# Probabilities transposed by the DMA crossbar instead of by TensorE, in a windowed-attention plus rational-MLP kernel

## The chip, the cores and the metric

The kernel runs on one core of a Trainium2 chip. The metric is the device time of one execution in microseconds (us). The core has TensorE (PE, with its weight loads as PEld), VectorE (DVE), ScalarE (ACT), GpSimd (POOL), SyncE (SP, which here only issues transfers) and 16 DMA engines.

## The reference

Eight sequences of 576 positions, eight heads of width 64, a causal window of 128 keys with a linear bias; then a two-layer network whose activation is a ratio of polynomials.

```python
scores = scale * np.matmul(q, k.transpose(0, 1, 3, 2))
rel = pos[:, None] - pos[None, :]
mask = (rel >= 0) & (rel < 128)
scores = np.where(mask, scores + bias[None], -1000000000.0)
attn = np.exp(scores - np.max(scores, axis=-1, keepdims=True))
attn = attn / (np.sum(attn, axis=-1, keepdims=True) + 1e-09)
x = np.matmul(attn, v)                  # to (4608 tokens, 512)
h = x @ w_in                            # 512 x 2048
P = a[0] + a[1] * h + a[2] * h**2 + a[3] * h**3
Q = 1.0 + np.abs(b[0]) * np.abs(h) + np.abs(b[1]) * h**2
out = (P / (Q + 1e-6)) @ w_out          # 2048 x 512
```

## The kernel before

The 4608 tokens are cut into 18 tiles of 256. Each tile has two attention jobs (function `attention`, j = 0 to 35), one for each half of the heads; a job has two units (function `unit`, i = 0, 1), each with two heads and two blocks of 128 tokens. The MLP (function `mlp`) then takes the tile in 8 pairs of 128-wide slices of the hidden layer. Attention of the next tile stands between the matmuls of the MLP of this tile, so one tile holds two jobs. The stretch from one job to the next is called a half of a tile below.

A job begins on PE with one block of small matmuls: the value products of the job before (`side<-p_all` and `side<-p_far`, L397), then its own scores (`sc<-kq` and `side<-kq`, L444). DVE merges the scores (L468) and takes their maximum with the bias (L507), eight instructions in a job; ACT takes the exponentials (L512), eight in a job; DVE makes the reciprocal of the sum (L519, L520); POOL multiplies (`pr<-pr,st`, L521). PE then transposes the probabilities `pr` of a unit by four matmuls against an identity (L536) into PSUM, ACT copies them out (`p_all`, L539), and POOL splits them by two instructions into `p_far` (L543) and the rest (L544).

A pair of the MLP: PE makes `h` (L621); ACT makes `g_u` (L635) and `g_p` (L649); POOL makes `g_q` (L636, L650); ACT takes a logarithm (L653) and an exponential (L654); DVE makes `g_h` (L656) and `g_l` (L659), which PE multiplies with the second weights (`acc`, L676). Matmuls in three parts of fp32r keep the precision. In the first tile the weights still arrive as 64-bit floats, and ACT and DVE turn them into fp32 (L582 to L584).

No order is written by hand: every operation is handed to a list scheduler (`Plan`) with a due time from a table of numbers and a cost, and each engine's program is emitted in the order that it finds. Each engine then runs its list in that order, so an instruction that waits holds up those behind it. SP issues nearly all transfers, from one queue.

Of the kernel before, what the change touches and what calls it, by code (L numbers as in the profile page):

```python
# [15 lines left out]
U32 = mybir.dt.uint32  # L16
AF = mybir.ActivationFunctionType
# [18 lines left out]
EARLY = 0  # L36

# [42 lines left out]
class Plan:  # L80
# [34 lines left out]
    def order(self):  # L115
# [76 lines left out]
        while n < total:  # L192
# [12 lines left out]
            for e in "pavgsq":  # L205
                while free_at[e] <= t:
# [7 lines left out]
                    if best is None:  # L214
                        break
# [54 lines left out]
def banded_attention_ratio_mlp(ctx: ExitStack, tc: tile.TileContext, kqv, w_in, w_out, ab, bias, ident, out):  # L270
# [14 lines left out]
    A0, DA, T0, L0, L1 = -4.313, 1.223, 17.768, 62.357, 26.153  # L285
    AOFF, D2, D3, JL, VL = -0.7979, 3.783, 6.667, 12.545, 6.301
    SP, SV, SA, SG, LL = 0, 0.3731, 0.1218, 0.3643, 2.215
    ML, ZA, ME, OE, C0 = 25.673, 0.5894, 1.484, 12.272, 0.9828
    DC, CO, DO, WL, S0 = 4.041, 22.113, 3.584, 5.75, 81.852
    DS, SL, AW, BL, VE = 1.47, 9.066, 23.44, 0.2145, 5.594  # L290
    DU, V0, DL = 0.8139, 7.94, 1.703
# [11 lines left out]
    def act(n, psum, ptr=0):  # L303
        return (67 if psum else 105) + 0.833 * n + 95 * ptr
# [7 lines left out]
    masks = slot(const, [P, 2, P], F32, "masks")  # L312
    masks16 = slot(sb3, [P, 2, P], BF16, "masks16", tag="p_far")
# [44 lines left out]
    def job(j, i):  # L358
# [24 lines left out]
    stage = {}  # L383

# [34 lines left out]
    def attention(j):  # L419
# [4 lines left out]
        side = [slot(ps4, [P, 2, 2, P], F32, f"side{h}", tag="h") for h in range(2)]  # L424
# [6 lines left out]
        extra = lambda h: ap(side[h])[:, 0].rearrange("q i (b c) -> q i b c", b=2)  # L431
# [14 lines left out]
        if t == 0:  # L446
            for i in range(2):
                plan.op(A + DU * i, {"p": 290 + 664}, lambda e, i=i: scores(i), reads=jobs[i][3], writes=mk + [(side[0], 0), (side[1], 0)], rows=0.9)
# [18 lines left out]
        for h in range(2):  # L467
# [4 lines left out]
                reads=[mk[h], (side[h], 0), (masks, 0)], writes=[mk[h]])  # L472
# [10 lines left out]
    def unit(j, i, A, main, mk, pt, v):  # L483
# [54 lines left out]
        plan.op(A + D2, {"p": 28 + 108 * 4}, transpose, reads=[(pr, y) for y in range(4)] + [(id_sb, 0)], writes=pk)  # L538
# [243 lines left out]
```

## Time and profile before

| | |
|---|---|
| time, median of 3 runs (lowest to highest) | 999.61 us (999.29 to 1000.06) |
| time of the profiled execution | 999.67 us |
| its span | 997.9 us |
| busy: PE, DVE, ACT, POOL | 98%, 79%, 61%, 53% |

The profiled execution lies 0.06 us above the median, and its span 1.8 us below its time. The engines work at the same time, so the shares don't add up; a busy PE can still have matmuls that overlap.

### The profile page before, as it was taken

The page shows a single profiled execution, that of the slowest core. Times are in us where ns is not written, and L with a number is a line of the kernel's source. Part 1 is how long each engine was busy: PE and PEld are TensorE (multiplying, and loading weights), DVE is VectorE, ACT ScalarE, POOL GpSimd, SP SyncE. Part 2 cuts the span into 40 slices and gives each one's busy share as a digit, 9 for nine tenths or more (in the row PEclk, how much of TensorE's full clock was granted, in tenths as well). Part 3 has the DMA queues.
Part 4 walks back from the last instruction along what each step waited for, and adds up shares of the span by engine and source line. Part 5 has one row for each costly group of instructions (what it writes and reads, how often), then busy time and mean ns, then how long its engine had stood idle before and what let it go on. Part 6 is the DMA issues. An engine that isn't in the chain of part 4 may idle for free.

```text
span 997.9 us, 25220 instructions
## 1 busy us (share of the span) xinstructions
PE 976.8 (98%) x9999; PEld 867.0 (87%) x9999; DVE 791.6 (79%) x1786; ACT 611.6 (61%) x1410; POOL 525.4 (53%) x529
## 2 busy tenths in 40 slices
PE   6899899999999999999999999999999999999998
PEld 4756698999999999999999999999999999999997
DVE  5799997887878787877787877878787878777775
ACT  5798865665656566655656565656566565656452
POOL 3448984555555554554545454555555545545332
PEclk7899999999999999999999999999999999999999
DMA  9991311121112112121212131203021221200000
GB/s 283 366 325 26 95 48 60 50 94 41 62 51 74 56 54 70 49 75 55 70 49 75 39 96 45 79 2 102 22 80 44 55 75 54 71 1 22 2 22 22
DMA packets 54502, 73.86 MB, mean 74 GB/s; under 512 B 5488, under 2 KB 38512, under 8 KB 54384
## 3 DMA queue, kind: packets, MB, share of 16 engines
q1 hardware_dynamic: 53664, 71.59, 22.9%
q8 instruction: 79, 1.29, 0.6%
q10 hardware_dynamic: 720, 0.66, 0.2%
q14 instruction: 39, 0.32, 0.1%
HBM read 62.79 MB, written 9.44 MB: 72 GB/s over the span
## 4 chain that ended last, share of the span: by engine, by line
PE 91%; DVE 3%; DMA 3%; ACT 1%; issue 1%; SPq 0%; ACTq 0%; DVEq 0%
PE h L621 40%; PE acc L676 39%; PE side L397 5%; PE sc L536 3%; PE sc L444 3%; PE side L444 1%; DMA v<-in_kqv 1%; DVE w L584 1%; DMA kq<-in_kqv 1%; DMA raw<-in_w_in 1%; DMA bias_std<-in_bias 1%; ACT pr L512 0%; DVE cv L583 0%; DVE g_q L644 0%; DVE g L647 0%
## 5 line engine op out<-in xcount | busy, mean ns | idle before, releaser
L621 PE MATMUL h<-x_hi,hi 128*128 128x256 f32 x1088 | 313.6, 288 | 0.0
L621 PE MATMUL h<-x_hi,lo 128*128 128x256 f32 x1088 | 306.2, 281 | 0.0
L621 PE MATMUL h<-x_lo,hi 128*128 128x256 f32 x1088 | 306.0, 281 | 0.0
L636 POOL TENSOR_SCALAR g_q<-g_u,babs 128x512 f32<-128x512 f32 x144 | 123.2, 855 | 252.8 <-ACT g_u L635 252.1
L621 PEld LDWEIGHTS h<-x_lo,hi 128*128 128x128 f32 x1088 | 204.7, 188 | 43.1 <-issue 1.0
L621 PEld LDWEIGHTS h<-x_hi,hi 128*128 128x128 f32 x1088 | 205.3, 189 | 25.4 <-issue 0.7
L676 PE MATMUL acc<-lo,g_h 128*128 128x512 f32 x544 | 214.7, 395 | 0.0
L676 PE MATMUL acc<-hi,g_h 128*128 128x512 f32 x544 | 214.5, 394 | 0.0
L676 PE MATMUL acc<-hi,g_l 128*128 128x512 f32 x544 | 207.7, 400 | 0.0
L621 PEld LDWEIGHTS h<-x_hi,lo 128*128 128x128 f32 x1088 | 204.9, 188 | 0.0
L650 POOL TENSOR_TENSOR g_q<-g_q,g_u 128x512 f32<-128x512 f32 x136 | 175.9, 1293 | 11.0
L521 POOL TENSOR_TENSOR pr<-pr,st 128x512 f32<-128x512 f32 x72 | 76.0, 1055 | 178.8 <-DVE st L520 128.6
L656 DVE SCALAR_TENSOR_TENSOR g_h<-h,ab_sb,g_u 128x512 fp32r<-128x512 f32 x136 | 101.9, 749 | 80.4 <-ACT g_u L654 79.4
L653 ACT ACTIVATE g_u<-g_q,fixed 128x512 f32<-128x512 f32 x136 | 98.0, 720 | 90.8 <-POOL g_q L650 90.7
L512 ACT ACTIVATE pr<-pr,st 128x128 f32<-128x128 f32 x288 | 112.6, 392 | 48.7 <-DVE st L507 48.7
L635 ACT ACTIVATE g_u<-h 128x512 f32<-128x512 f32 x144 | 86.0, 597 | 59.6 <-PE h L621 56.2
L649 ACT ACTIVATE g_p<-h,ab_sb 128x512 f32<-128x512 f32 x136 | 105.5, 778 | 18.0 <-PE h L621 17.9
L651 DVE TENSOR_TENSOR g_p<-h,g_p 128x512 f32<-128x512 f32 x136 | 93.7, 689 | 27.2 <-ACT g_p L649 23.4
L657 DVE SCALAR_TENSOR_TENSOR g_q<-g_q,g_h 128x512 f32<-128x512 f32 x136 | 97.7, 718 | 12.8
L658 DVE SCALAR_TENSOR_TENSOR h<-h,ab_sb,g_q 128x512 f32<-128x512 f32 x136 | 102.9, 756 | 3.5
L676 PEld LDWEIGHTS acc<-hi,g_h 128*128 128x128 f32 x544 | 102.6, 189 | 2.1
L652 DVE SCALAR_TENSOR_TENSOR h<-g_p,ab_sb,h 128x512 f32<-128x512 f32 x136 | 102.1, 751 | 2.5 <-ACT g_u L635 0.3
(75 smaller groups left out, 1516.6 us busy)
## 6 DMA issues: line engine op xcount, KB each, us to landing
kq<-in_kqv SPq DMA_DIRECT2D x72, 320.0 KB, 3.8
v<-in_kqv SPq DMA_DIRECT2D x144, 128.0 KB, 3.9
out<-o SPq DMA_DIRECT2D x34, 256.0 KB, 2.0
raw<-in_w_in SPq DMA_DIRECT2D x16, 512.0 KB, 8.6
raw<-in_w_out SPq DMA_DIRECT2D x16, 512.0 KB, 8.6
bias_t<-in_bias SPq DMA_DIRECT2D x44, 64.0 KB, 2.0
out<-o SPq DMA_DIRECT2D x4, 128.0 KB, 1.8
bias_first<-in_bias ACTq DMA_DIRECT2D x1, 256.0 KB, 4.6
```

The lines of the kernel that those rows point to most:

```text
L512: nc.scalar.activation(ap(pr)[:, :, y, :], ap(pr)[:, :, y, :], AF.Exp, bias=ap(st)[:, y : y + 1], scale=-1.0, accum_out=ap(st)[:, 4 + y : ...
L621: nc.tensor.matmul(h(n), w[:, k, :], x[:, k, :], start=(k == 0 and m == 0), stop=(k == NKC - 1 and m == len(seq) - 1))
L636: plan.op(E, {"g": tsc}, lambda e: nc.gpsimd.tensor_scalar(v(g_q), v(g_u), ap(babs)[:, 1:2], ap(babs)[:, 0:1], ALU.mult, ALU.add), reads=[ ...
L649: plan.op(E, {"a": act(W, 1, 2) - 20}, lambda e: nc.scalar.activation(v(g_p), v(h_s), AF.Identity, bias=ap(ab_sb)[:, 2:3], scale=ap(ab_sb) ...
L650: plan.op(E, {"g": ttc}, lambda e: nc.gpsimd.tensor_tensor(v(g_q), v(g_q), v(g_u), ALU.mult), reads=[(g_q, 0), (g_u, 0)], writes=[(g_q, 0) ...
L651: plan.op(E, {"v": dve(W)}, lambda e: nc.vector.tensor_tensor(v(g_p), v(h_s), v(g_p), ALU.mult), reads=[(h_s, 0), (g_p, 0)], writes=[(g_p, ...
L652: plan.op(E, {"v": dve(W, 1)}, lambda e: stt(v(h_s), v(g_p), ap(ab_sb)[:, 1:2], v(h_s), ALU.add, ALU.mult), reads=[(h_s, 0), (g_p, 0), (ab ...
L653: plan.op(E, {"a": act(W, 0, 1)}, lambda e: nc.scalar.activation(v(g_u), v(g_q), AF.Ln, bias=guard, scale=1.0), reads=[(g_q, 0)], writes=[ ...
L656: plan.op(E, {"v": dve(W, 1)}, lambda e: stt(v(g_h), v(h_s), ap(ab_sb)[:, 0:1], v(g_u), ALU.add, ALU.mult), reads=[(h_s, 0), (g_u, 0), (ab ...
L657: plan.op(E, {"v": dve(W)}, lambda e: stt(v(g_q), v(g_q), GUARD, v(g_h).bitcast(F32), ALU.add, ALU.mult), reads=[(g_q, 0), (g_h, 0)], writ ...
L658: plan.op(E, {"v": dve(W, 1)}, lambda e: stt(v(h_s), v(h_s), ap(ab_sb)[:, 0:1], v(g_q), ALU.add, ALU.subtract), reads=[(h_s, 0), (g_q, 0), ...
L676: nc.tensor.matmul(ap(accs[t][i]), x[:, sl], w, start=(c == 0 and part == 0 and m == 0), stop=(c == NFC - 1 and part == parts - 1 and m == ...
```

## The change

From job 6 on (the fourth tile) the probabilities of a unit, 128 x 512 fp32, are no longer transposed on PE. ACT copies them into two planes of 16-bit halves (`planes`, 128 x 1024), SP issues one transposing DMA from SBUF to SBUF (`turned`), and ACT puts the halves together again in `p_all`. The 60 copies out of PSUM (L539) fall away with the 240 transposes. POOL's two splits stay there; jobs 0 to 4 get theirs from PSUM directly by one ACT copy and two DVE multiplications with a mask (`near`, `far`), in place of a copy and two POOL instructions. In the first tile both jobs share the side tiles, DVE may take the multiplication L521, the loads of keys and queries come ahead of those of the values, and PE is filled with idle matmuls (`warming`) until 23.9 us. In the second tile ACT may take L636. The table of due times is new throughout.

```diff
@@ the scheduler, an idle PE in the first 23.9 us
-                        break
+                        if e != "p" or self.fill is None or not self.fill[0] <= t < self.fill[1] or self.fill[2].turn is None:
+                            break
+                        o, spot = Op(), self.fill[2]
...
@@ the table, two lines of eight
-    A0, DA, T0, L0, L1 = -4.313, 1.223, 17.768, 62.357, 26.153
-    AOFF, D2, D3, JL, VL = -0.7979, 3.783, 6.667, 12.545, 6.301
+    A0, DA, T0, L0, L1 = -18.311, 0.8259, 19.833, 64.972, 26.934
+    AOFF, D2, D3, JL, VL = -0.8613, 3.942, 7.183, 11.989, 5.931
...
@@ unit
-        plan.op(A + 1.2, {"g": 185 + 1.6 * 4 * P}, lambda e: nc.gpsimd.tensor_tensor(
+        plan.op(A + 1.2, {"g": 185 + 1.6 * 4 * P, "v": dve(4 * P)} if j < 2 else {"g": 185 + 1.6 * 4 * P}, lambda e: eng[e].tensor_tensor(
...
-        plan.op(A + D2, {"p": 28 + 108 * 4}, transpose, reads=[(pr, y) for y in range(4)] + [(id_sb, 0)], writes=pk)
-        plan.op(A + D2 + 0.2, {"a": act(4 * P, 1), "v": dve(4 * P)} if j < 3 else {"a": act(4 * P, 1)}, ...)
+        if j >= TURNED:
+            planes = slot(sb2, [P, 2, 4 * P], U16, "planes")
+            turned = slot(sb2, [P, 8, P], U16, "turned")
+            plan.op(A + 1.4, {"a": act(8 * P, 0)}, lambda e: nc.scalar.copy(ap(planes), ap(pr).rearrange("q k y c -> q (k y c)").bitcast(U16).rearrange("q (x s) -> q s x", s=2)),
+                    reads=[(pr, y) for y in range(4)], writes=[(planes, 0)])
+            plan.op(A + D4, {"s": 1300}, lambda e: eng[e].dma_start_transpose(ap(turned), ap(planes).rearrange("q s x -> q (s x)")), reads=[(planes, 0)], writes=[(turned, 0)])
+            plan.op(A + D2 + 0.2, {"a": act(8 * P, 0)}, lambda e: nc.scalar.copy(ap(w)[:, : 4 * P].bitcast(U16).rearrange("q (x s) -> q s x", s=2), ap(turned).rearrange("q (s g) x -> q s (g x)", s=2)),
+                    reads=[(turned, 0)], writes=[(w, 0)])
+        else:
+            plan.op(A + (D2 if t else D0), {"p": 28 + 108 * 4}, transpose, reads=[(pr, y) for y in range(4)] + [(id_sb, 0)], writes=pk)
...
+        if j < DIRECT:
+            picked = lambda y: slant(pt(), y)
+            sides = lambda m: m.rearrange("q (k c) -> q k c", k=2)[:, :, None].to_broadcast([P, 2, 2, 64])
+            T = A + (D2 if t else D0) + 0.2
+            plan.op(T, {"a": act(2 * P, 1)}, lambda e: nc.scalar.copy(fresh(1), picked(1)), reads=pk, writes=[(w, 1)])
+            plan.op(T, {"v": dve(2 * P)}, lambda e: nc.vector.tensor_tensor(fresh(0), picked(0), sides(ap(near)), ALU.mult), reads=pk + [(near, 0), (near, 1)], writes=[(w, 0)])
+            plan.op(T, {"v": dve(2 * P)}, lambda e: nc.vector.tensor_tensor(ap(w2), picked(0), sides(ap(masks)[:, 1]), ALU.mult), reads=pk + [(masks, 0)], writes=[(w2, 0)])
+            return
...
@@ mlp
-        plan.op(E, {"g": tsc}, lambda e: nc.gpsimd.tensor_scalar(v(g_q), v(g_u), ...
+        plan.op(E, {"g": tsc, "a": act(W, 0, 2) - 20} if t == 1 else {"g": tsc},
```

On ACT, the order of one half of a tile in the steady part of the program stood as follows before: the eight exponentials of a job come in two groups, and behind each the copy `p_all` out of PSUM (`sc`) of a unit.

```order
L512 ACTIVATE pr_5379,st_5380<-pr_5379,st_5380 128x2x64 x4
L653 ACTIVATE g_u_5360<-g_q_5372,fixed_76 128x512
L654 ACTIVATE g_u_5360<-g_u_5360 128x512
L635 ACTIVATE g_u_5426<-h_5356 128x512
L649 ACTIVATE g_p_5430<-h_5356,ab_sb_104 128x512
L539 COPY p_all_5443<-sc_5309 128x512
L512 ACTIVATE pr_5449,st_5450<-pr_5449,st_5450 128x2x64 x4
L653 ACTIVATE g_u_5426<-g_q_5437,fixed_76 128x512
L654 ACTIVATE g_u_5426<-g_u_5426 128x512
L635 ACTIVATE g_u_5510<-h_5422 128x512
L649 ACTIVATE g_p_5516<-h_5422,ab_sb_104 128x512
L539 COPY p_all_5532<-sc_5309 128x512
```

In the changed program such a half (the second of its tile) stands on ACT as follows, behind its eight exponentials; L678, L694, L698 and L699 are the lines L635, L649, L653 and L654 of before.

```order
L563 COPY planes_8791<-pr_8711 128x1024
L678 ACTIVATE g_u_8801<-h_8715 128x512
L694 ACTIVATE g_p_8808<-h_8715,ab_sb_111 128x512
L678 ACTIVATE g_u_8814<-h_8722 128x512
L563 COPY planes_8820<-pr_8726 128x1024
L694 ACTIVATE g_p_8832<-h_8722,ab_sb_111 128x512
L698 ACTIVATE g_u_8801<-g_q_8812,fixed_76 128x512
L566 COPY p_all_8851<-turned_8803 128x2x512
L699 ACTIVATE g_u_8801<-g_u_8801 128x512
L698 ACTIVATE g_u_8814<-g_q_8840,fixed_76 128x512
L566 COPY p_all_8876<-turned_8834 128x2x512
L699 ACTIVATE g_u_8814<-g_u_8814 128x512
```

The exponentials of both units now stand together, and each copy `p_all<-turned`, which waits for a transfer, stands ahead of an exponential L699 of the MLP.

On SP, the two transfers of that half stand between loads and outputs; each row names the semaphores that it waits for (the one of ACT is that of `planes`).

```order
L393 DMA kq_8592<-in_kqv 128x640 [waits DMAHW7_49,PE_49]
L391 DMA v_8596<-in_kqv 64x2x256 [waits DMAHW0_49]
L391 DMA v_8596<-in_kqv 64x2x256 [waits DMAHW1_49]
L750 DMA out_0<-o_8557 128x512 [waits DMAHW2_49,Activation_49]
L565 DMA_TRANSPOSE turned_8803<-planes_8791 128x8x128 [waits DMAHW3_49,Activation_49]
L565 DMA_TRANSPOSE turned_8834<-planes_8820 128x8x128 [waits DMAHW4_49,Activation_49]
L522 DMA bias_t_8861<-in_bias 128x256 [waits DMAHW5_49,DVE_49]
L522 DMA bias_t_8874<-in_bias 128x256 [waits DMAHW6_49,DVE_49]
```

The six rows around the two transposing ones are moves of before; behind the transposing ones wait bias tables and the next loads.

On PE, the end of the same half holds the first matmuls that read `g_h_8872`, the result of the first L699 above.

```order
L664 MATMUL h_8883<-x_hi_7995,hi14_1670 128x256
L664 MATMUL h_8883<-x_lo_8004,hi14_1670 128x256
L664 MATMUL h_8883<-x_hi_7995,lo14_0_1723 128x256
L721 MATMUL acc0_8568<-hi8_1354,g_h_8872 128x512
L721 MATMUL acc0_8568<-lo8_1_1403,g_h_8872 128x512
L664 MATMUL h_8883<-x_hi_7995,hi14_1670 128x256
```

Between the start of that half's value block and the first of these L721 rows the order has 32 matmuls of L721 (`acc`, L676 before) and 75 of L664 (`h`, L621 before), and up to the second pair's `g_h_8901` 44 and 96; in the first half of a tile the two counts are 32 and 93, and again 44 and 96. Up to the next value block it is 48 and 96. No transpose stands in between any more.

## Rows read from the trace of the kernel before

**Rows 1.** The page, busy time of each engine over the span, with share and instructions.
```profile
PE 976.8 (98%) x9999; PEld 867.0 (87%) x9999; DVE 791.6 (79%) x1786; ACT 611.6 (61%) x1410; POOL 525.4 (53%) x529
```

**Rows 2.** The page, the chain that ended last: shares of the span by engine, then by line.
```profile
PE 91%; DVE 3%; DMA 3%; ACT 1%; issue 1%; SPq 0%; ACTq 0%; DVEq 0%
PE h L621 40%; PE acc L676 39%; PE side L397 5%; PE sc L536 3%; PE sc L444 3%; PE side L444 1%; DMA v<-in_kqv 1%; DVE w L584 1%; DMA kq<-in_kqv 1%; DMA raw<-in_w_in 1%; DMA bias_std<-in_bias 1%; ACT pr L512 0%; DVE cv L583 0%; DVE g_q L644 0%; DVE g L647 0%
```

**Rows 3.** Windows: from, to, length, busy us by engine (instructions), PEclk, DMA share, GB/s.
```profile
145.01:914.00 768.99, 768.85 (x8244) 698.71 (x8245) 608.67 (x1410) 461.97 (x1085) 400.83 (x409) 1.00 0.19 58
...
245.19:298.07 52.88, 52.88 (x565) 48.06 (x568) 41.73 (x97) 31.70 (x74) 27.51 (x28) 1.00 0.18 59
```

**Rows 4.** Timeline of PE: start us, duration us, engine, line, operation, tiles, count.
```profile
277.78 0.29 PE L621 MATMUL h<-x_hi,lo 128*128 128x256 f32 x1
277.90 0.60 PE L536 MATMUL sc<-id_sb,pr 128*128 128x128 f32 x4
...
278.46 0.28 PE L621 MATMUL h<-x_lo,hi 128*128 128x256 f32 x1
```

**Rows 5.** The same timeline, 11 us earlier, where a values-and-scores block stands.
```profile
266.30 0.67 PE L397 MATMUL side<-p_all,v 64*64 64x128 f32 x16
...
269.14 0.73 PE L676 MATMUL acc<-hi,g_l 128*128 128x512 f32 x2
...
270.17 0.28 PE L621 MATMUL h<-x_hi,hi 128*128 128x256 f32 x1
...
270.52 0.39 PE L676 MATMUL acc<-hi,g_h 128*128 128x512 f32 x1
...
270.98 0.28 PE L621 MATMUL h<-x_hi,hi 128*128 128x256 f32 x1
```

**Rows 6.** Groups of ACT, POOL and DVE: count, busy us, mean ns, idle before them.
```profile
L654 ACT ACTIVATE g_u<-g_u 128x512 f32<-128x512 f32 x136 | 85.8, 631 | 3.7
...
L539 ACT COPY p_all<-sc 128x512 f32<-128x512 f32 x68 | 40.0, 588 | 51.6 <-PE sc L536 51.6
L415 ACT CAST x_hi<-side 128x256 fp32r<-128x256 f32 x68 | 22.1, 376 | 80.8 <-PE side L444 78.1 <-PE side L397 2.2 <-DVE sc L468 0.5
...
L583 ACT ACTIVATE cv<-raw,fixed 128x512 int32<-128x512 uint32 x14 | 10.2, 733 | 1.7 <-DVE w L584 1.7
...
L650 POOL TENSOR_TENSOR g_q<-g_q,g_u 128x512 f32<-128x512 f32 x136 | 175.9, 1293 | 11.0
L636 POOL TENSOR_SCALAR g_q<-g_u,babs 128x512 f32<-128x512 f32 x144 | 123.2, 855 | 252.8 <-ACT g_u L635 252.1 <-DVE g L647 0.7
L521 POOL TENSOR_TENSOR pr<-pr,st 128x512 f32<-128x512 f32 x72 | 76.0, 1055 | 178.8 <-DVE st L520 128.6 <-ACT g_u L653 39.2 <-issue 7.0
L543 POOL TENSOR_TENSOR p_far<-p_all,masks 128x256 f32<-128x256 f32 x72 | 61.3, 852 | 10.6 <-ACT p_all L539 9.3 <-DVE p_all L539 1.0
...
L652 DVE SCALAR_TENSOR_TENSOR h<-g_p,ab_sb,h 128x512 f32<-128x512 f32 x136 | 102.1, 751 | 2.5 <-ACT g_u L635 0.3
```

**Rows 7.** Timelines of DVE and ACT in one half of a tile.
```profile
250.48 0.29 DVE L507 CUSTOM_DVE_ANT_0 pr<-sc,bias_std 128x128 f32<-128x128 f32 x1
...
250.69 0.28 DVE L507 CUSTOM_DVE_ANT_0 pr<-sc,bias_std 128x128 f32<-128x128 f32 x1
...
250.81 0.40 ACT L512 ACTIVATE pr<-pr,st 128x128 f32<-128x128 f32 x1 [0.91 <-DVE st L507]
```

**Rows 8.** DMA: packets, MB, share of 16 engines (85 to 96 us); issues, KB, us to landing.
```profile
q1 hardware_dynamic: 288, 0.13, 4.0%
...
bias_t<-in_bias SPq DMA_DIRECT2D x2, 64.0 KB, 1.9
...
out<-o SPq DMA_DIRECT2D x26, 256.0 KB, 2.1
```

**Rows 9.** Windows of the start, columns as in Rows 3.
```profile
0.00:35.00 35.00, 23.37 (x368) 18.05 (x369) 20.90 (x85) 19.47 (x66) 13.62 (x20) 0.76 1.01 298
35.00:125.00 90.00, 84.54 (x707) 60.89 (x706) 83.83 (x160) 77.84 (x160) 62.36 (x55) 1.00 0.55 189
```

More of the change, by code (lines that the diff above doesn't have):

```diff
@@ L36 @@
 EARLY = 0
+DIRECT = 5
+TURNED = 6
 def block_type(n):
@@ L214, in order @@
                     if best is None:
-                        break
+                        if e != "p" or self.fill is None or not self.fill[0] <= t < self.fill[1] or self.fill[2].turn is None:
+                            break
+                        o, spot = Op(), self.fill[2]
+                        o.due, o.engines, o.emit, o.after, o.rows, o.sb = 0.0, {"p": 108}, self.fill[3], 0.0, 1.0, False
+                        o.deps, o.slots, o.users, o.follows, o.engine, o.left = set(), [spot], [], (), e, 0
+                        spot.left.append(o)
+                        spot.open += 1
+                        best = [t, 0.0, 0, o]
+                        ready[e].append(best)
+                        n -= 1
                     o = best[3]
@@ L312, in banded_attention_ratio_mlp @@
     masks = slot(const, [P, 2, P], F32, "masks")
+    near = slot(const, [P, P], F32, "near")
     masks16 = slot(sb3, [P, 2, P], BF16, "masks16", tag="p_far")
@@ L332, in constants @@
         plan.op(-7, {"v": 300}, lambda e: nc.vector.tensor_copy(ap(masks), ap(masks16)), reads=[(masks16, 0)], writes=[(masks, 0)])
+        for k in range(2):
+            c, o = slice(64 * k, 64 * k + 64), slice(64 - 64 * k, P - 64 * k)
+            plan.op(-7, {"v": 140}, lambda e, c=c, o=o: nc.vector.tensor_copy(ap(near)[:, c], ap(masks16)[:, 1, o]), reads=[(masks16, 0)], writes=[(near, k)])
         plan.op(10, {"v": 70}, lambda e: nc.vector.tensor_scalar_mul(ap(na), ap(ab_sb)[:, 0:4], -1.0), reads=[(ab_sb, 0)], writes=[(na, 0)])
@@ L423, in attention @@
         back = j - 1 if j > 2 else None
-        side = [slot(ps4, [P, 2, 2, P], F32, f"side{h}", tag="h") for h in range(2)]
+        if j != 1:
+            shared[:] = [slot(ps4, [P, 2, 2, P], F32, f"side{h}", tag="h") for h in range(2)]
+        side, n = list(shared), 1 if j == 1 else 0
         if j == 1:
@@ L447, in attention @@
             for i in range(2):
-                plan.op(A + DU * i, {"p": 290 + 664}, lambda e, i=i: scores(i), reads=jobs[i][3], writes=mk + [(side[0], 0), (side[1], 0)], rows=0.9)
+                plan.op(A + DU * i, {"p": 290 + 664}, lambda e, i=i: scores(i), reads=jobs[i][3], writes=mk + [(side[0], n), (side[1], n)], rows=0.9)
         else:
@@ L711, in banded_attention_ratio_mlp @@
     ones = nc.const_aps.tensor(1.0, [P, 512], BF16)
-    for j in range(7):
-        plan.op(-9, {"p": 216}, lambda e, j=j: nc.tensor.matmul(ap(warm), ones[:, :P], ones, start=(j == 0), stop=(j == 6)), writes=[(warm, 0)], after=600)
-    for j in range(8):
-        plan.op(-9, {"p": 108}, lambda e: nc.tensor.matmul(ap(warm)[:, :256], ones[:, :P], ones[:, :256], start=True, stop=True), writes=[(warm, 0)], after=3617.319 + 500.0 * j)
+    warming = lambda e: nc.tensor.matmul(ap(warm)[:, :256], ones[:, :P], ones[:, :256], start=True, stop=True)
+    plan.op(-30, {"p": 108}, warming, writes=[(warm, 0)], after=600)
+    plan.op(-30, {"p": 108}, warming, writes=[(warm, 0)], after=1000 * FE)
+    plan.fill = (600, 1000 * FE, warm, warming)
     for j in range(3):
```

52 lines of the change are left out of this document (31 added, 21 removed).

## The prediction

> **What bounds the kernel now.** I read the page's busy line first: PE 98%, the next engine, DVE, 79% [rows 1]. The chain that ended last confirms it: PE holds 91% of it, nearly all in the two matmul lines of the MLP, and the transposes L536 have 3% [rows 2]. Then the windows, to see whether this holds everywhere: from 145 to 914 us PE is busy for 768.85 of 768.99 us at a granted clock of 1.00, and in one tile of 52.88 us DVE is busy for 41.73, ACT for 31.70, POOL for 27.51 [rows 3]. So in this stretch an instruction taken from PE shortens the span by its full price, as long as nothing on the other engines comes too late. The start is another regime: up to 35 us PE is busy for two thirds at a mean clock of 0.76 while the DMA engines are full, and from 35 to 125 us PE is busy for 84.54 of 90, DVE for 83.83 [rows 9].
>
> **Prices on PE.** Matmuls overlap, so I take the distance from start to start. A plain `h` matmul: (270.52 - 270.17) / 3 = 0.117 us. An `acc` matmul: (270.98 - 270.52) / 2 = 0.23. A block of values and scores: 269.14 - 266.30 = 2.84 [rows 5]. Around the four transposes of a unit the start goes from 277.90 to 278.46, and that contains one plain matmul: 0.56 - 0.12 = 0.44 us for a block of four [rows 4]. Check: a tile has 96 `acc`, 192 `h`, two blocks and four transpose blocks, 22.1 + 22.5 + 5.7 + 1.8 = 52.1, against 52.88 measured; I scale the PE times below by 1.015.
>
> **What the change removes.** Jobs 6 to 35 have 60 units: 60 x 0.44 = 26.4 us off PE. That is the main term. A tile would go from 52.88 to 51.1.
>
> **What it adds.** Per unit, two ACT copies of 1024 elements replace one of 512. No row has 1024 elements. From 256 to 512 elements a copy grows from 376 to 588 ns, 0.83 ns each; from SBUF 512 cost 631; so 631 + 512 x 0.83 = 1.06 us [rows 6]. Whether 16-bit elements four bytes apart go at this rate no row tells: below I take 1.06, above twice that, 2.1 us. The nearest is the conversion to integers, 733 instead of 631 for 512 elements, which would make 1.23; I take 1.1. ACT's load per tile rises by 4 x (2.2 - 0.59) = 6.4 to 38 of 51 us, so ACT does not become the bound; but it runs in order, and what counts is lateness.
>
> The transfer: 256 KB inside SBUF. From below, a store of the same size lands 2.1 us after issue. For the pieces: two bias tables, 288 packets of about 512 B, took 4.0% of 16 engines' 11 us, 24 ns each, and landed after 1.9 us [rows 8]. With 18 packets per engine that is 0.44 us of packets and 1.5 of fixed time. If the transposition moves rows of 256 B, 1024 of them, it is 64 x 24 ns + 1.5 = 3.0 us; if it works in pieces of 32 B, 512 per engine, 12.3 + 1.5 = 13.8 us. I take 3.0, since all transfers of this size in the rows lie near it, and keep 13.8 as the upper end.
>
> **Is it hidden?** I put zero at the start of the value block and go through the changed order of the second half of a tile. Before, the first maximum comes at 250.48 - 245.19 = 5.3, the first exponential at 5.6 [rows 3, 7]. Now all eight maxima follow each other at 0.21, until 7.0, and the eight exponentials at 0.40 until 8.8. DVE has three long instructions (0.75 each) and two short ones (0.2) up to the first reciprocal: 9.6. POOL's product takes 1.05: 10.7. `planes` 1.1: 11.9, and the first transfer is issued. ACT goes on with three MLP instructions (0.6 each), then the second `planes`: 14.8, second transfer. POOL meanwhile has the second product until 13.1, then L636 and L650 (0.86, 1.29): 15.3; the logarithm ends at 16.0, and `p_all` could start at 16.1. So 16.1 - 11.9 = 4.2 us of the first transfer are hidden outright. Behind `p_all` (1.1) stand the exponential (0.63), DVE's `g_h` (0.75) and three hand-overs of 0.1: `g_h` at 18.9. PE wants it after 2.84 + 32 x 0.23 + 75 x 0.117 = 19.0, scaled 19.3. Margin 0.4, so a transfer of up to 4.6 us costs nothing here. In the first half of a tile PE wants it after 93 instead of 75 `h`, at 21.4: margin 2.5, up to 6.7 us. The second `p_all` starts after POOL's next pair (17.5) and the logarithm at 18.2, 3.4 us behind its issue; its `g_h` is there at 21.0 and wanted at 24.5, the values after two splits (0.85 each) at about 21.2 and wanted 25.5. Up to 6.9 us that is free. With 3.0 us nothing is late, and the term is zero. What the copies and the wait are hidden by is thus the time between a pair's `h` and its use; if the first `p_all` is late by more than 0.4 us, the next thing late is `g_h`, and PE waits.
>
> A reader of the Trainium skill would be warned here. Its page "VectorE: DVE Perf Modes", section "The three transpose paths", gives 1309 ns for a 128 x 128 bf16 transposition by the crossbar and 390 ns on TensorE, and its rules prefer TensorE where PSUM will do as the target. Here PSUM did, and the four on PE cost 0.44 us by the rows, not four times 390 ns. If the eight blocks of a transfer cost 8 x 1.309 = 10.5 us, an estimate from that page, the transfers would come far too late; no row here shows a crossbar transfer.
>
> **The start.** Each of jobs 0 and 1 loses, in its last unit, a copy of 0.59 and two splits of 0.85 in favour of a DVE pair of 256 elements, about 0.42 each (half of 0.75 and a fixed part): 2.3 - 0.8 = 1.5 us shorter each [rows 6]. The filler raises the clock of a PE that is not the bound there. From 35 us DVE is nearly full; it gains four units of jobs 3 and 4 (8 x 0.42 = 3.4 us) and hands six conversions to ACT and POOL (4.5). Of the 3 us I count half, 1.5, because full DMA engines set when weights arrive [rows 9]. Bounds: 6 us gained if all of it and the slow clock come back, 4 lost if the new load order delays weights.
>
> **Sum.** 999.67 - 26.4 - 1.5 + 0 = 971.8, and 0.06 less against the median: 972 us.
>
> **Rivals.** (a) The transfer lands late, the other side: between 4.6 and 6.7 us only every second half loses, above that every one. 27.9 = 15 (L - 4.6) + 15 (L - 6.7) gives L = 6.6 us as the point from which the kernel is slower. At 13.8 us the second transfer queues behind the first and lands at 11.9 + 13.8 + 12.3 = 38.0 where 21.7 would do: 30 x 16.3 = 489, so 1461 us. For it speaks that no such transfer is in the trace; against it, that all known ones of 64 to 256 KB take about 2 us. The page's 10.5 us is this same rival: the second lands at 32.9, 11.2 late in each half, 1308 us. (b) The transfer is in time, but ACT is slow on 16-bit halves: at 1.6 us a copy, the three copies up to `g_h` come 1.5 later, 1.1 beyond the margin in 15 halves: 16 us back, 988. The same half of the gain goes with a transfer of 5.7 us. At 2.1 the 3.0 us cost 15 x 2.6 + 15 x 0.5 = 47, and it belongs to (a). (c) PE's time is not what sets the pace, or the start gives everything back: no change. The windows speak against it: DVE has 41.73 us of work for a tile of 51.1 [rows 3].
>
> **Chances.** Forecast (965 to 978) 0.55; part of the gain lost, as in (b), 978 to 997.6, 0.22; better than 965, 0.02; (c), within 0.2% (about what a measurement can tell from no change), 0.03; (a) or slow copies, slower, 0.18. To leave out no more than 2 in 10 the range goes from 965 up to 1002, the unknown latency making it that wide; the forecast's own range is 965 to 978. Faster 0.79, same 0.03, slower 0.18.
>
> **What would show it.** A tile of 51.1 us in the windows, PE at 100% there, no wait of PE on `g_h` or `p_all`; copies of 1.06 to 1.2 us; transfers landing within 4.6 us. Wrong: ACT idle ahead of `p_all<-turned` with the DMA as releaser and PE waiting for DVE's `g_h` in each second half, or a first matmul on fp32r parts of the second tile that starts later than before.

## The result and the profile after

The changed kernel takes 982.57 us (median of 4 runs, 981.69 to 984.04) beside 999.45 us (999.27 to 1000.06) for the kernel before: a ratio of 0.9831 [0.9814, 0.9849], 16.9 us faster. The forecast was 972 us with a range of 965 to 1002, so the direction and the range held, and the kernel lies 10.6 us above the number. The profiled execution took 982.69 us, with a span of 980.9.

The page of the changed kernel, with the lines that answer to [rows 1] and [rows 2]:

```profile
PE 963.7 (98%) x9871; PEld 847.1 (86%) x9871; DVE 779.5 (79%) x1802; ACT 701.2 (71%) x1482; POOL 503.0 (51%) x503
...
PE 71%; DVE 12%; ACT 11%; issue 3%; DMA 2%; POOL 0%; ACTq 0%; DVEq 0%
```

PE is still the fullest engine, but the chain that ended last tells another story than before: PE's share fell from 91% to 71%, and DVE and ACT, which had 4% together, now have 23%. The kernel is one in which PE waits in places. The windows show which (columns as in [rows 3]):

```profile
0.00:35.00 35.00, 31.37 (x481) 25.30 (x482) 23.48 (x86) 17.24 (x55) 3.32 (x7) 1.00 0.96 297
35.00:125.00 90.00, 86.10 (x728) 62.72 (x727) 83.77 (x182) 85.25 (x189) 57.24 (x48) 0.98 0.63 196
145.01:890.00 744.99, 739.34 (x7810) 664.33 (x7803) 588.24 (x1385) 536.16 (x1126) 390.64 (x401) 1.00 0.32 79
```

Before, PE was busy for all but 0.14 us of the long stretch; now it lacks 5.65 us of 745. PE's waits from 140 to 940 us name the places (what waited, for what, us in all, times, longest); before, this view was empty:

```profile
PE h L664 <- DVE x_lo L436: 2.6, 5, 0.6
PE acc L721 <- ACT o L749: 1.8, 1, 1.8
PE acc L721 <- DVE g_h L701: 0.7, 1, 0.7
PE acc L721 <- DVE g_l L704: 0.3, 1, 0.3
```

Here `x_hi` and `x_lo` are the two fp32r parts of the attention's result, which `h` is made of, and `o` is the copy of a tile's finished sums out of PSUM. L417, L435, L436, L490 and L749 are the lines L397, L415, L416, L468 and L704 of before. The list comes to 5.4 us, less than half of what will turn out to be lost.

The new instructions themselves, by line (duration as least/median/most ns, then first and last start, and shape), beside the 588 ns of the copy out of PSUM in [rows 6] and the 2.1 us of a store in [rows 8]:

```profile
L563 ACT COPY planes<-pr x60: 1030/1047/1063, 155.0 to 914.9; 128x1024 uint16<-128x1024 uint16 x60
...
L565 SPq DMA_TRANSPOSE turned<-planes x60: 1232/1270/1942, 156.1 to 916.0; - x60
DMA to landing us min/median/max: 3.0/3.1/5.0
...
L566 ACT COPY p_all<-turned x60: 1335/1365/1399, 159.2 to 919.6; 128x1024 uint16<-128x1024 uint16 x60
its engine sat idle before it (us, times) until:
  DMA turned<-planes: 5.0, 8
```

The transfer lands after 3.1 us, as taken, and `planes` takes 1.05 us. The merge `p_all<-turned` takes 1.37 us and not 1.1: `planes` reads its 16-bit elements four bytes apart and writes them in a row, the merge reads in a row and writes four bytes apart.

Two of the waits can be followed in timelines. The first is the longest, ahead of 528 us, at the end of the ninth tile; ACT's rows, then PE's (a bracket gives the idle time ahead of the instruction and what ended it):

```profile
522.15 1.36 ACT L566 COPY p_all<-turned 128x1024 uint16<-128x1024 uint16 x1
523.37 0.63 ACT L699 ACTIVATE g_u<-g_u 128x512 f32<-128x512 f32 x1
523.90 0.72 ACT L698 ACTIVATE g_u<-g_q,fixed 128x512 f32<-128x512 f32 x1
524.51 1.37 ACT L566 COPY p_all<-turned 128x1024 uint16<-128x1024 uint16 x1
525.74 0.62 ACT L699 ACTIVATE g_u<-g_u 128x512 f32<-128x512 f32 x1
526.26 1.43 ACT L694 ACTIVATE g_p<-h,ab_sb 128x512 f32<-128x512 f32 x2
527.59 1.07 ACT L749 COPY o<-acc 128x512 f32<-128x512 f32 x2
```

```profile
522.92 0.63 PE L721 MATMUL acc<-hi,g_l 128*128 128x512 f32 x2
528.22 0.50 PE L721 MATMUL acc<-hi,g_h 128*128 128x512 f32 x1 [1.82 <-ACT o L749]
```

PE finished the tile's sums at 523.5 and has `h` matmuls until 526.4. The output copies `o`, which free the accumulators for the next tile, stand on ACT behind two merges, three other instructions and two `g_p`; ACT works without a pause and reaches them at 527.59. The second kind is behind a block of values and scores (DVE, ACT, PE):

```profile
248.88 0.75 DVE L701 SCALAR_TENSOR_TENSOR g_h<-h,ab_sb,g_u 128x512 fp32r<-128x512 f32 x1 [0.52 <-ACT g_u L699]
...
250.35 0.69 DVE L490 COPY_PREDICATED sc<-masks,side 128x512 f32<-128x512 uint32 x1
251.75 0.70 DVE L490 COPY_PREDICATED sc<-masks,side 128x512 f32<-128x512 uint32 x1 [0.71 <-ACT x_hi L435]
252.36 0.75 DVE L436 TENSOR_TENSOR x_lo<-side,x_hi 128x256 fp32r<-128x256 f32 x2
...
251.07 0.65 ACT L435 CAST x_hi<-side 128x256 fp32r<-128x256 f32 x2 [0.52 <-DVE sc L490]
...
252.92 0.35 PE L664 MATMUL h<-x_hi,hi 128*128 128x256 f32 x1 [0.50 <-DVE x_lo L436]
```

DVE's first merge reads one side tile, ACT's `x_hi` waits for it, DVE's second merge waits for `x_hi`, and only then comes `x_lo`, for which PE waits. The two engines hand the side tiles to each other and back. ACT is not behind at `x_hi`: it sits idle for 0.5 us until DVE's merge ends. But DVE comes to that merge behind `g_h`, for which it had waited 0.52 us for ACT's exponential L699; that ACT's lateness gets here in this way is read from this one place. ACT's `x_hi` waits for DVE's merge in 15 halves of tiles, while PE's list has five waits for `x_lo`; the view of `x_hi` (L435):

```profile
its engine sat idle before it (us, times) until:
...
  DVE sc L490: 7.8, 15
```

Before, ACT's `x_hi` sat idle for this merge for 0.5 us in all [rows 6].

### The profile page after: what moved, and what is told of

Its sections match the earlier page's. It is cut to its first block, busy times and chain, and to the rows that moved or that the text cites. A ratio compares the mean times of both kernels' runs of the same rounds, so it can differ in the third digit from the quotient of the medians.

```text
span 980.9 us, 25130 instructions
## 1 busy us (share of the span) xinstructions
PE 963.7 (98%) x9871; PEld 847.1 (86%) x9871; DVE 779.5 (79%) x1802; ACT 701.2 (71%) x1482; POOL 503.0 (51%) x503
## 3 DMA queue, kind: packets, MB, share of 16 engines
q1 hardware_dynamic: 117024, 87.32, 33.4%
## 4 chain that ended last, share of the span: by engine, by line
PE 71%; DVE 12%; ACT 11%; issue 3%; DMA 2%; POOL 0%; ACTq 0%; DVEq 0%
PE h L664 32%; PE acc L721 31%; PE side L417 4%; PE sc L466 2%; DVE g_h L701 2%; ACT g_u L699 1%; DVE g_q L702 1%; DMA turned<-planes 1%; ACT g_u L678 1%; ACT g_u L698 1%; DVE g_l L704 1%; DVE h L703 1%; DVE g_p L696 1%; ACT pr L534 1%; PE side L466 1%
## 5 line engine op out<-in xcount | busy, mean ns | idle before, releaser
L664 PE MATMUL h<-x_hi,hi 128*128 128x256 f32 x1088 | 309.7, 285 | 2.8 <-DVE x_lo L436 2.6
L664 PE MATMUL h<-x_hi,lo 128*128 128x256 f32 x1088 | 306.6, 282 | 0.0
L664 PE MATMUL h<-x_lo,hi 128*128 128x256 f32 x1088 | 306.6, 282 | 0.0
L664 PEld LDWEIGHTS h<-x_lo,hi 128*128 128x128 f32 x1088 | 205.8, 189 | 25.0 <-issue 1.2
L664 PEld LDWEIGHTS h<-x_hi,hi 128*128 128x128 f32 x1088 | 206.0, 189 | 23.4 <-issue 9.7
L721 PE MATMUL acc<-hi,g_h 128*128 128x512 f32 x544 | 215.7, 396 | 2.5 <-ACT o L749 1.8
L721 PE MATMUL acc<-lo,g_h 128*128 128x512 f32 x544 | 214.3, 394 | 0.0
L543 POOL TENSOR_TENSOR pr<-pr,st 128x512 f32<-128x512 f32 x71 | 80.5, 1134 | 257.4 <-DVE st L542 138.0
L664 PEld LDWEIGHTS h<-x_hi,lo 128*128 128x128 f32 x1088 | 206.1, 189 | 0.0
L721 PE MATMUL acc<-hi,g_l 128*128 128x512 f32 x544 | 193.1, 400 | 0.4 <-DVE g_l L704 0.3
L695 POOL TENSOR_TENSOR g_q<-g_q,g_u 128x512 f32<-128x512 f32 x136 | 178.6, 1316 | 14.7 <-ACT g_q L680 5.7
L680 POOL TENSOR_SCALAR g_q<-g_u,babs 128x512 f32<-128x512 f32 x136 | 109.1, 803 | 138.8 <-ACT g_u L678 132.2
L701 DVE SCALAR_TENSOR_TENSOR g_h<-h,ab_sb,g_u 128x512 fp32r<-128x512 f32 x136 | 101.4, 747 | 51.1 <-ACT g_u L699 50.9
L678 ACT ACTIVATE g_u<-h 128x512 f32<-128x512 f32 x144 | 85.7, 597 | 75.1 <-DVE g_p L696 35.5
L694 ACT ACTIVATE g_p<-h,ab_sb 128x512 f32<-128x512 f32 x136 | 105.7, 779 | 43.8 <-PE h L664 43.7
L698 ACT ACTIVATE g_u<-g_q,fixed 128x512 f32<-128x512 f32 x136 | 98.3, 723 | 33.6 <-POOL g_q L695 33.4
L721 PEld LDWEIGHTS acc<-hi,g_h 128*128 128x128 f32 x544 | 102.5, 188 | 14.0 <-ACT o L749 2.0
L721 PEld LDWEIGHTS acc<-lo,g_h 128*128 128x128 f32 x544 | 102.2, 188 | 11.0
L721 PEld LDWEIGHTS acc<-hi,g_l 128*128 128x128 f32 x544 | 99.2, 189 | 11.4 <-DVE g_l L704 0.8
```

The source lines that it names most:

```text
L543: plan.op(A + 1.2, {"g": 185 + 1.6 * 4 * P, "v": dve(4 * P)} if j < 2 else {"g": 185 + 1.6 * 4 * P}, lambda e: eng[e].tensor_tensor(ap(pr) ...
L664: nc.tensor.matmul(h(n), w[:, k, :], x[:, k, :], start=(k == 0 and m == 0), stop=(k == NKC - 1 and m == len(seq) - 1))
L678: plan.op(E, {"a": act(W, 1)}, lambda e: nc.scalar.activation(v(g_u), v(h_s), AF.Abs), reads=[(h_s, 0)], writes=[(g_u, 0)])
L680: lambda e: nc.scalar.activation(v(g_q), v(g_u), AF.Identity, bias=ap(babs)[:, 0:1], scale=ap(babs)[:, 1:2]) if e == "a" else nc.gpsimd.te ...
L694: plan.op(E, {"a": act(W, 1, 2) - 20}, lambda e: nc.scalar.activation(v(g_p), v(h_s), AF.Identity, bias=ap(ab_sb)[:, 2:3], scale=ap(ab_sb) ...
L695: plan.op(E, {"g": ttc}, lambda e: nc.gpsimd.tensor_tensor(v(g_q), v(g_q), v(g_u), ALU.mult), reads=[(g_q, 0), (g_u, 0)], writes=[(g_q, 0) ...
```

## The experiments

Theory A: what was lost are waits that ACT's backlog makes, through copies that are longer than taken. Theory B: the waits come from the order that the new table makes. Theory C: the transfer is late after all.

**Everything but the transposition.** `start_only`:

```diff
-TURNED = 6
+TURNED = 99
```

> All probabilities are transposed by TensorE as before, and everything else of the change stays (first tile, direct splits of jobs 0 to 4, idle matmuls, new table). This leaves out the main term of -25.7 us and the 16-bit copies. Theory A (waits come from the copies): what is left is the start, -0.6 us by the traces and -1.5 by the prediction, so 998 to 999 us and a tile of 52.9 us. Theory B (the new table makes the waits): 9 us of waits stay, about 1008 us, with PE waiting for x_lo and the accumulators as in the changed kernel.

995.17 us, 0.9961 [0.9948, 0.9975]: 3.9 us faster than before, more than either theory gave. Its window (columns as above):

```profile
145.00:890.00 745.00, 745.00 (x7977) 676.20 (x7971) 596.89 (x1372) 448.15 (x1058) 382.73 (x399) 1.00 0.20 59
```

PE waits nowhere from 145 us on, so the new table by itself makes no waits. The order is another one than in the changed kernel, though, since the scheduler plans anew without the transfers. On top of `start_only` the transposition is worth 995.17 - 982.57 = 12.6 of the 26.4 us that its price on PE promises; 995.2 - 26.4 = 968.8 is what the kernel would take without a wait, and the changed one lies 13.8 us above that.

Where they lie can be read from the fourth block of value products, which stands ahead of the first transfer. Its first rows in the kernel before, `start_only`, the changed kernel and `mended` (below):

```profile
144.94 0.67 PE L397 MATMUL side<-p_all,v 64*64 64x128 f32 x16
142.24 0.67 PE L417 MATMUL side<-p_all,v 64*64 64x128 f32 x16
143.88 0.67 PE L417 MATMUL side<-p_all,v 64*64 64x128 f32 x16
143.16 0.67 PE L417 MATMUL side<-p_all,v 64*64 64x128 f32 x16
```

From there on the last three have the same matmuls left, 3072 of `h`, 1568 of `acc` and 31 blocks, but for the 60 blocks of transposes. The changed kernel gets there 143.88 - 142.24 = 1.6 us later than `start_only`. From there to the end of its span it takes 980.9 - 143.9 = 837.0 us and `start_only` 993.2 - 142.2 = 851.0: 14.0 of 26.4 us are gained, and 12.4 are lost on the way.

PE's list of waits names 5.4 us of them. A matmul that starts late while the row of the one before it still lasts shows no idle time: rows of `acc` are 0.39 us long and follow each other at 0.23 [rows 5]. Equal halves of tiles show more of it. In the changed kernel twelve halves in a row, with 96 matmuls of `h`, 48 of `acc` and a block each, go from 532.10 to 845.26 us, 313.2 us. In `mended` equal halves follow each other at 25.52 us from 554.80 on, which makes 306.2. Of these 7.0 us the list names about 3. The twelve are among the 15 halves in which `x_hi` waits for DVE's merge.

**The merge, shorter in the same order.** `merge_in_order`, same result:

```diff
-ap(w)[:, : 4 * P].bitcast(U16).rearrange("q (x s) -> q s x", s=2), ap(turned).rearrange("q (s g) x -> q s (g x)", s=2)
+ap(w)[:, : 4 * P].bitcast(U16).rearrange("q (x s) -> q x s", s=2), ap(turned).rearrange("q (s g) x -> q (g x) s", s=2)
```

> The second copy of each unit (p_all<-turned) reads its 16-bit elements four bytes apart and writes them one behind the other, instead of the other way round; same result, same order on every engine. In the changed kernel that copy took 1367 ns, and the other copy, which reads apart and writes in order, 1047 ns. Theory A (the 9.3 us that PE waits come from ACT falling behind through the long copies): the copy falls to about 1.05 us, ACT has 60 x 0.32 = 19 us less to do, the waits ahead of the accumulator at 528 us (two such copies ahead of the released output copies, 0.6 us) and for g_h shrink, and the time goes from 982.6 to 977 to 980. Theory B (the waits come from the order that the new table makes, as x_lo behind two merges on DVE): the copy falls too, but the time stays within 1 us of 982.6. If the direction of the stride is not what made the copy long, it stays at 1.37 us and so does the time.

978.47 us, 0.9796 [0.9783, 0.981]. The merge by line:

```profile
L566 ACT COPY p_all<-turned x60: 1152/1173/1198, 159.3 to 915.1; 128x1024 uint16<-128x1024 uint16 x60
```

0.19 us less a copy, 11.5 us of ACT's time, gave 4.1 us, within what A gave, though the copy did not reach 1.05 us. `short_merge` then cut it to one plane:

```diff
-ap(w)[:, : 4 * P].bitcast(U16).rearrange(...), ap(turned).rearrange("q (s g) x -> q s (g x)", s=2)
+ap(w)[:, : 4 * P], ap(turned).rearrange("q s x -> q (s x)")[:, 4 * P :]
```

> The copy p_all<-turned is cut to one of its two planes: it reads 512 16-bit numbers in order and writes them as fp32, and the other half of the bits is left out. It still waits for the transfer, and the order on every engine is that of the changed kernel. A plain copy of 512 elements from SBUF took 0.63 us, so ACT would have 60 x 0.74 = 44 us less to do. Theory A (PE's waits come from ACT's long copies): cutting 0.19 us of each copy gave 4.1 us, so cutting 0.74 should give back nearly all of the 12 to 13 us by which the changed kernel lies above the kernel with TensorE's transposes minus their price (995.2 - 26.4 = 968.8): 969 to 973 us. Theory C (what is late is the transfer, not the copy): 978 us or more, with ACT's waits for the transfer longer than the 5.0 us of now, since it reaches the copies earlier.

975.04 us, 0.9763 [0.9749, 0.9776], outside of what either theory gave. Its merge by line:

```profile
L566 ACT CAST p_all<-turned x60: 602/621/641, 159.4 to 913.5; 128x512 f32<-128x512 uint16 x60
its engine sat idle before it (us, times) until:
  DMA turned<-planes: 9.0, 12
```

The first 0.19 us gave 4.1, the next 0.55 only 3.4 more; 6.2 us above 968.8 stay. ACT now waits for the transfer more often, 9.0 us, and PE still waits for `x_lo` and an output copy (2.6 us in 5 places). So the length of the copies alone is not the cause.

**The order of a few instructions.** `mended` is `merge_in_order` with two kinds of moves on ACT: in the 15 jobs in which DVE's first merge comes ahead of `x_hi`, the two halves of `x_hi` change places, and in the ninth tile the two output copies go ahead of two `g_p`. `order_only` has the moves with the long merge.

```diff
...
     order = plan.order()
+    for j, (x, y) in high.items():
+        m, n = order.index(x), order.index(y)
+        if (j, 0) in first and order.index(first[j, 0]) < m:
+            order[m], order[n] = y, x
+    on_act = [o for o in order if o.engine == "a"]
+    ahead = on_act[on_act.index(outs[8, 0]) - 2]
+    for i in range(2):
+        order.remove(outs[8, i])
+        order.insert(order.index(ahead), outs[8, i])
...
```

`high` holds a job's two `x_hi`, `first` DVE's merges L490, `outs` the output copies.

> The copy with the stride on its reads (978.5 us), and two moves in the order: where the first predicated merge on DVE stands ahead of x_hi, ACT copies the other half of x_hi first, so that the two engines don't read the same side tile; and in the ninth tile the two output copies stand ahead of the two g_p that they stood behind on ACT. Theory A with B as a second cause (order at single places adds to ACT's lateness): the 2.4 us that PE waits for x_lo in 5 places and the 1.5 us that it waits for an output copy go: 974 to 975 us. Rival (a wait taken away at one place comes back at the next, since ACT is late as a whole): 977 to 978.5 us.

> The two moves in the order (x_hi's other half first, two output copies ahead of two g_p) without the change of the stride: the copy p_all<-turned takes 1.37 us again. Shorter copies alone gave 4.1 us and the moves on top of them 5.3. If the two causes are independent: 982.6 - 5.3 = 977.3 us. If the moves only help where the copies are short, since ACT is otherwise late by more than a move gives: 980 to 982.6 us. If ACT's lateness makes every badly placed instruction dearer: below 976.5 us.

`mended` takes 973.15 us, 0.9743 [0.973, 0.9757], a little below its theory's 974 to 975, and `order_only` 975.42, 0.9762 [0.9749, 0.9776]. PE's waits in `mended`, 140 to 940 us, and its window:

```profile
PE acc L721 <- DVE g_l L704: 0.3, 1, 0.3
PE acc L721 <- ACT o L749: 0.2, 1, 0.2
```

```profile
145.01:890.00 744.99, 744.40 (x7836) 672.38 (x7829) 594.21 (x1395) 534.88 (x1135) 397.01 (x407) 1.00 0.31 80
```

PE is full again. The moves gave 7.2 us with the long merge and 5.3 with the short one; the short merge gave 4.1 in the old order and 2.3 with the moves. So the two causes take part in the same waits, and misplaced instructions cost more where ACT is late, the third case of the expectation; the runs of a kernel spread by 1.3 to 2.4 us, so that these 1.8 us are less certain than the gains themselves. Both kernels beat the changed one, `mended` by 9.4 us. The twelve halves that took 313.2 us take 308.5 in `order_only` (529.66 to 838.18) and 307.1 in `mended` (528.41 to 835.49): most of what the moves gave comes from `x_hi`.

**A new order.** The scheduler found one twice: in `true_cost` the new table stayed and it was told a truer cost of the merge; `turned_old_table` is the kernel before, with the old table, and the transposing branch of the change alone (planes, transfer, merge).

```diff
-plan.op(A + D2 + 0.2, {"a": act(8 * P, 0)}, lambda e: nc.scalar.copy(...),
+plan.op(A + D2 + 0.2, {"a": 1230}, lambda e: nc.scalar.copy(...),
```

> The list scheduler is told 1230 ns for the copy p_all<-turned in place of its 958, and finds another order; the kernel's instructions stay the same. Theory A: orders that count on a copy of 0.96 us are what makes ACT late (the copy takes 1.37 us); with a truer cost the exponentials and output copies stand where ACT can reach them, and 3 to 6 of the 9.3 us of PE's waits go: 977 to 980 us. Theory B (the table's due times, fitted with the old cost, matter more): the new order has waits of its own at other places, 980 to 988 us.

> The kernel before with one part of the change alone: from job 6 on the probabilities go through planes, transfer and merge as in the changed kernel, with the old table of due times, and the list scheduler finds the order by the old numbers (p_all without its padding, so that the new tiles fit). By the prediction's sum, which took the gain from PE's price alone: 999.1 - 26.4 = 973 us. If the order must be found anew for the later copies, as the run with the true cost suggests (1001.9 us with the new table): 985 to 1005 us, with PE waiting for g_h, g_l and the values.

1001.85 us, 1.0031 [1.002, 1.0043], and 1001.55, 1.0024 [1.0014, 1.0033]. The first lies outside of both expectations: with the same instructions, 19.3 us slower than the changed kernel. The second lies in the range for an order that must be found anew. The longest of PE's waits from 140 to 940 us, of `true_cost`, then of `turned_old_table`:

```profile
PE side L417 <- issue: 9.4, 11, 1.3
PE h L664 <- DVE g_l L704: 3.1, 2, 1.7
PE acc L721 <- DVE g_l L704: 3.0, 9, 0.8
```

```profile
PE acc L689 <- DVE g_h L669: 6.6, 2, 3.7
PE h L634 <- DVE g_l L672: 3.3, 2, 1.8
```

Two orders of the same instructions lie 26.4 us apart (975.42 in `order_only`, 1001.85 in `true_cost`), as much as the whole price of the transposition on PE.

**The transfer.** `merge_from_planes` and `mended_from_planes` copy from the transfer's source (the second reads the two planes alternately, as `mended` does):

```diff
-ap(turned).rearrange(...)
+ap(planes)
```

> The copy p_all<-turned reads planes, the transfer's source, in place of its result; the transposition is left out of the result, but each transfer still runs, and the copy is as long as before (1.37 us, stride on the writes). Nothing waits for the transfer any more. Theory A (the copies' length on ACT makes the waits): only the 5.0 us that ACT waits for transfers in 8 places go, and of these a part reaches PE: 979 to 982.6 us. Theory C (the transfer's latency is what is late): most of the 13 us come back, 970 to 974 us.

> The faster kernel of the last group (973.2 us: stride on the reads, two moves), with p_all copied from planes in place of the transfer's result; each transfer still runs, the transposition is left out of the result. It tells what waiting for the transfer is still worth. ACT waited there for transfers 3.3 us in 6 places, PE for almost nothing (0.5 us). Theory A (the waits were ACT's lateness, and that is gone): 972 to 973.2 us. Theory C (the latency of the transfer delays ACT as a whole): 969 to 971 us.

978.86 us, 0.9798 [0.9785, 0.9812], at the edge of theory A's 979, and 973.03, 0.9738 [0.9725, 0.9752], as theory A had it. In the changed kernel's order the wait for the transfer is worth 3.7 us; in the mended order 0.1, which is nothing. C holds only as a third share in the same waits.

`transfer_twice` makes it later:

```diff
-lambda e: eng[e].dma_start_transpose(ap(turned), ...)
+lambda e: [eng[e].dma_start_transpose(ap(turned), ...) for _ in range(2)]
```

> Each transposing transfer is issued twice from the same queue, the second writing the same bytes again; the copy p_all<-turned waits for both. One transfer lands 3.1 us after its issue; two should land after 4.4 (if they overlap and only the issue of 1.27 us is added) to 6.2 us (one behind the other). Prediction's margins (4.6 us in the second half of a tile, 6.7 in the first): at 4.4 us nothing is lost, 983 us; at 6.2 us 15 x 1.6 = 24 us, 1007 us. Rival: in the trace the copy starts 3.8 us (median) behind the end of planes, so the slack is already used up by ACT's order; then each unit's copies come late by 0.6 to 2.4 us and PE loses that in each of 30 halves: 1000 us at 4.4 us, 1055 at 6.2.

1153.07 us, 1.1546 [1.1517, 1.1576], 98 us above the higher figure. SP's rows, then ACT's, in one half of a tile:

```profile
312.83 4.33 SPq L565 DMA_TRANSPOSE turned<-planes  x2
...
318.57 4.32 SPq L565 DMA_TRANSPOSE turned<-planes  x2
...
311.76 1.05 ACT L563 COPY planes<-pr 128x1024 uint16<-128x1024 uint16 x1 [1.83 <-POOL pr L543]
...
314.34 1.05 ACT L563 COPY planes<-pr 128x1024 uint16<-128x1024 uint16 x1
...
318.97 1.36 ACT L566 COPY p_all<-turned 128x1024 uint16<-128x1024 uint16 x1 [1.61 <-DMA turned<-planes]
...
324.73 1.35 ACT L566 COPY p_all<-turned 128x1024 uint16<-128x1024 uint16 x1 [2.49 <-DMA turned<-planes]
```

ACT's wait for it in all, and the page's busy line:

```profile
ACT p_all L566 <- DMA turned<-planes: 146.8, 60, 4.8
```

```profile
PE 1013.9 (88%) x9871; PEld 884.1 (77%) x9871; DVE 781.1 (68%) x1802; ACT 703.9 (61%) x1482; POOL 498.8 (43%) x503
```

The second transfer writes the same tile, so the program makes it wait for the first by a semaphore, and SP with it. So the first unit's result is there 318.97 - 312.81 = 6.2 us behind the end of its `planes`, the second's 324.73 - 315.39 = 9.3. If all halves were like this one, the prediction's margins (4.6 us for the first unit in every second half, 6.9 for the second unit) would give 15 x 1.6 + 30 x 2.4 = 96 us; it is 1153.1 - 982.6 = 170.5. The two profiled executions, whose spans lie 1147.6 - 980.9 = 166.7 us apart, tell the parts. PE is idle for 1147.6 - 1013.9 = 133.7 us instead of 980.9 - 963.7 = 17.2, 116.5 more. The other 50.2 are longer busy time of the same matmuls (1013.9 against 963.7), at a mean granted clock of 0.953 instead of 0.998; 0.045 x 1148 = 52 us is what that clock would make. So the pauses alone are 20 us more than the margins give, and the clock that fell with them makes the rest.

**The start.** `no_filler`:

```diff
-            o.emit(o.engine)
+            if o.emit is not warming or o in plan.ops:
+                o.emit(o.engine)
```

> The idle matmuls that fill PE until 23.9 us are left out; the order of all other instructions stays. The granted clock was 0.76 on average up to 35 us before the change and 1.00 after it. Theory of the prediction (PE is not what the first 35 us wait for, so its clock is worth little): within 1 us of 982.6. Rival (the 1 to 2 us that the first two tiles have gained come from the clock): 984 to 986 us, with the first output 1 to 2 us later.

982.28 us, 0.9836 [0.9822, 0.9849]: the idle matmuls do nothing for the time. What they do to the clock stays open. The window of the profiled execution:

```profile
0.00:35.00 35.00, 21.78 (x354) 17.78 (x355) 23.39 (x86) 16.93 (x55) 3.32 (x7) 1.00 0.93 296
```

PE is busy for 21.78 us without them, no more than the 23.37 of before, and the granted clock is 1.00 and not 0.76 [rows 9]. But the mean clocks over the span of the four executions of `no_filler` are 1.000, 0.991, 0.995 and 1.000; the changed kernel has 0.997 to 1.000 in its four, the kernel before 0.991 to 0.995 in 14. So without the idle matmuls the clock was as high as with them in two executions and as low as before in two, and these two took 983.16 and 982.43 us beside 982.13 and 982.07.

## Why the prediction was right, and where it was off

- **The main term**, 26.4 us for 60 blocks of four transposes, was right as a price. A tile was predicted at 51.1 us. Two blocks of value products in `mended` that lie a tile apart:

```profile
554.80 0.67 PE L417 MATMUL side<-p_all,v 64*64 64x128 f32 x16
...
605.85 0.67 PE L417 MATMUL side<-p_all,v 64*64 64x128 f32 x16
```

  605.85 - 554.80 = 51.05, and so it goes on to 835.49; in `start_only` it is 52.85, in the changed kernel, from 532.10 to 845.26, 51.5 to 53.0. Over the whole program the median falls by 22.0 us from `start_only` to `mended`, 4.4 less than the price. Of these 0.9 lie ahead of the fourth block (143.16 - 142.24). From there on `mended` takes 971.1 - 143.2 = 827.9 us, 23.1 less than `start_only`, so 3.3 are lost, all but a little ahead of 554.80; which instructions lose them was not taken apart.
- **The copies**: 1.06 to 1.1 us was right for `planes` (1.047), and low for the merge (1.367). The working asked whether 16-bit elements four bytes apart keep the rate, and had one price for reading and for writing them. By rival (b)'s own count, three copies up to `g_h`, this makes 2 x 1.047 + 1.367 - 3.3 = 0.16 us, less than the 0.4 of margin, and nothing would have been lost. Yet 0.19 us of each merge were worth 4.1 us.
- **The transfer**: 3.0 taken, 3.1 measured. The way to it was right too: the profile's page counts 117,024 packets on queue q1 after and 53,664 before, 1,056 for each of the 60 transfers, close to the 1024 rows of 256 B that it took and far from 32-byte pieces. Its "all known ones of 64 to 256 KB take about 2 us" was a wrong reading: the profile's page of before has 3.9 us for the loads of `v`, 128 KB. The estimate of 10.5 us from the Trainium skill's "VectorE: DVE Perf Modes", section "The three transpose paths", does not hold for eight blocks in one transfer, and the measurement decides. The Trainium skill's "Advanced Engine Details and Errata", section "X-Bar Transpose (TRN2)", says that such transfers are as fast as regular ones; 3.1 us beside 2.1 for a store of that size [rows 8] comes nearer to that.
- **"Is it hidden?", with its term of zero**, is the step that failed. Its margins were worked out for one half of a tile on its own, from the merge to `g_h`. In the order of an engine lateness goes on to instructions that the working never named: on ACT the output copies that free the accumulators, and on ACT and DVE `x_hi` and `x_lo`, which share the side tiles with DVE's merges. For `g_h` itself the margin was no bad guess (PE waits for it once, 0.7 us); the waits are at the end of a tile and, most of all, behind the value blocks. So neither of the signs of being wrong that it named, ACT idle ahead of `p_all<-turned` (5.0 us) and PE waiting for `g_h` in each second half, points at the place. In place of zero the term was 12.4 us. Single cures gave 4.1 (stride), 7.2 (moves) and 3.7 (no wait for the transfer), 15.0 together, more than there was to get: they are shares in the same waits, and two of them leave nothing for the third (973.15 to 973.03).
- **The start**, 1.5 us taken: the kernel before has six `acc` (1.4 us) more to do at its fourth block than the others, so the same work is done at 146.3 us there, at 143.88 in the changed kernel and at 142.24 in `start_only`: 2.4 and 4.1 us gained. The second is as much as `start_only` gained as a whole (3.9). That the filler is worth nothing was right; whether it raises the clock stays open.
- **The chances**: the time fell into "part of the gain lost", 978 to 997.6 us, which had 0.22 beside 0.55 for the forecast. The range was wide for the sake of a latency that turned out as taken, and what it caught in fact was another loss, so that it held was luck. What the prediction left out is that the order itself is worth as much as the gain, as 1001.9 and 1001.6 us show; it followed one half of one tile and took the rest for the same.

## What to carry to other kernels

Work that moves off a full engine pays its whole price only if every engine that runs in order still reaches, in time, all that frees a buffer; so follow the longest-lived resource (here the accumulators) across a whole period, not just the next consumer. Where a scheduler re-plans, hold the order fixed to price one instruction, and look at the places where PE waits: moving a few instructions there gave more than a faster copy. Compare equal stretches of work too, since the list of waits named less than half of the loss. A cure for a wait is worth what is left of it, so measure cures together as well as alone.

## What the runs showed of the hardware

- A 16-bit copy of 1024 elements on ACT took 1047 ns with the stride on its reads, 1173 ns reading two planes alternately, and 1367 ns with the stride on its writes.
- A crossbar transfer of 256 KB between SBUF tiles landed after 3.1 us and held SP for 1.27 us; two in a row into the same tile, the second made to wait for the first, held SP for 4.33 us.
- The granted clock of the first 35 us was 0.76 in the profiled execution of before and 1.00 in that of `no_filler` with PE busy no longer (23.37 and 21.78 us); over the span `no_filler` had 1.000 in two executions and 0.991 and 0.995 in two. What decides it was not found.
- After pauses of 117 us more in all, the mean granted clock of `transfer_twice` was 0.953, and the same matmuls were busy for 1013.9 us instead of 963.7.
